# Alternating the next block's transposes with an output group, moving two f tiles ahead, and loading the first x tile in two parts

## The chip, the cores and the metric

One core of a Trainium2 chip. The metric is the device time of the kernel in microseconds, of one launch. The engines are PE (TensorE), PEld (its weight loads), DVE (VectorE), ACT (ScalarE), POOL (GpSimd) and SP (SyncE, which issues most loads and stores).

## The reference, cut to what matters

```python
w = softmax(weight_gen, axis=-1)                  # (8, 4096, 8 heads, 7 taps)
x_unf = windows of x over 7 tokens (6 before)     # (8, 4096, 7, 8, 24)
conv = einsum('bshk,bskhg->bshg', w, x_unf)       # 32768 tokens x 192
h = conv @ w_in                                   # 192 -> 2048
out = (h - tanh(h)) @ w_out                       # 2048 -> 192
```

## The kernel before

32 blocks of 1,024 tokens. GpSimd multiplies x by the seven taps ("products"), a DMA adds half of them to the others (the "accumulation"), PE transposes and sums the products into PSUM (L233), ScalarE copies that to `convT`. Then come 16 "f tiles" of the first matmul (L257); each lands in one of three PSUM buffers, from which ScalarE makes the tanh and VectorE the difference. Eight "output groups" of the second matmul (L289) run for the block before, one after every two f tiles. The transposes use the same three buffers as the f tiles.

```python
psum_h = ctx.enter_context(tc.tile_pool(name="psum_h", bufs=3, space=bass.MemoryType.PSUM))
...
def gemm1(n, f):                       # one f tile
    ph = psum_h.tile([P, 2, HT], FP32, name="ph", tag="ph")
    ...                                # 6 matmuls, 3 per row half
    last_act[0] = nc.scalar.activation(out=th[:], in_=ph_f, func=ACT.Tanh)
    last_sub[0] = nc.vector.tensor_sub(gt[:], ph_f, th[:])
...
for n in range(NTOT):
    if n + 3 < NTOT:
        load_wg(n + 3)
        load_x(n + 3)                  # waits until POOL has freed the tile
    for p in range(J):
        gemm1(n, 2 * p)
        gemm1(n, 2 * p + 1)
        if n >= 1:
            gemm2((n - 1) * J + p)     # 16 f tiles, two matmuls each
        ...
        if n + 1 < NTOT:
            if p == (6 if n > 0 else 7):
                conv(n + 1, (0, 1))    # transposes of two chunks
            if p == (6 if n > 1 else 7):
                conv(n + 1, (2,))      # and of the third
```

The softmax here doesn't subtract the row's maximum and nothing guards it: scores larger than these inputs give would overflow.

## Time and profile before

| | before |
|---|---|
| time, median (lowest to highest) | 770.57 us (770.43 to 771.18) |
| profiled span | 768.73 us |
| PE, DVE, ACT, POOL busy | 96, 85, 83, 90% |
| a good steady block | 22.63 us |
| blocks 1, 2, 3 | 25.55, 24.09, 24.38 us |

The four costliest groups of the page (line, engine, operation, output from inputs, shapes, count, then busy time in us and mean ns of one, then idle time of the engine before them and what ended it):

```profile
L269 DVE TENSOR_TENSOR gt<-ph,th 128x1024 bf16<-128x1024 f32 x512 | 602.8, 1219 | 93.3 <-ACT th L267 92.7
L267 ACT ACTIVATE th<-ph 128x1024 f32<-128x1024 f32 x512 | 497.2, 1022 | 65.7 <-PE ph L257 64.9
L257 PE MATMUL ph<-convT,w_in 64*128 64x512 bf16 x3072 | 382.1, 378 | 7.5 <-DVE gt L269 5.0
L289 PE MATMUL obank<-w_out,gt 64*128 64x192 bf16 x7936 | 374.6, 243 | 2.9 <-issue 2.1
```

DVE and ACT wait in total for each other and for PE (93 and 66 us); PE hardly waits for anybody, 7.5 us in its largest group. PE is the bound; GpSimd, 90% busy, comes next, and the two engines that wait have over 10% to spare. The durations of single matmuls (378 and 243 ns) overlap and say nothing of the rate; the rate is read from starts.

### The profile page before, as it was taken

The page shows a single profiled execution, that of the slowest core. Times are in us where ns is not written, and L with a number is a line of the kernel's source. Part 1 is how long each engine was busy: PE and PEld are TensorE (multiplying, and loading weights), DVE is VectorE, ACT ScalarE, POOL GpSimd, SP SyncE. Part 2 cuts the span into 40 slices and gives each one's busy share as a digit, 9 for nine tenths or more (in the row PEclk, how much of TensorE's full clock was granted, in tenths as well). Part 3 has the DMA queues.
Part 4 walks back from the last instruction along what each step waited for, and adds up shares of the span by engine and source line. Part 5 has one row for each costly group of instructions (what it writes and reads, how often), then busy time and mean ns, then how long its engine had stood idle before and what let it go on. Part 6 is the DMA issues. An engine that isn't in the chain of part 4 may idle for free.

```text
span 768.7 us, 32330 instructions
## 1 busy us (share of the span) xinstructions
PE 736.7 (96%) x14784; PEld 583.1 (76%) x14784; DVE 652.9 (85%) x595; ACT 640.8 (83%) x865; POOL 695.2 (90%) x290
## 2 busy tenths in 40 slices
PE   2799999999999999999999999999999999999997
PEld 2377787777777777788777777777778777787777
DVE  5987888888898888889888888888888988888883
ACT  1777878888888888888888888888888888888883
POOL 5999999999999999999999999999999999999100
PEclk9999999999999999999999999999999999999999
DMA  7823776555677555577655557765556765542412
GB/s 209 184 81 87 182 181 150 118 145 147 169 182 174 131 129 148 150 180 182 164 123 133 150 160 182 180 128 137 143 150 172 182 181 115 125 142 72 98 43 84
DMA packets 25847, 111.37 MB, mean 145 GB/s; under 512 B 4800, under 2 KB 9456, under 8 KB 21624
## 3 DMA queue, kind: packets, MB, share of 16 engines
q1 hardware_dynamic: 14688, 76.95, 29.9%
q0 software_dynamic: 10816, 31.99, 25.8%
q8 instruction: 115, 1.88, 1.0%
q10 hardware_dynamic: 208, 0.39, 0.2%
q14 instruction: 20, 0.16, 0.1%
HBM read 54.49 MB, written 25.17 MB: 104 GB/s over the span
## 4 chain that ended last, share of the span: by engine, by line
PE 93%; DVE 2%; issue 1%; POOL 1%; DMA 1%; ACT 1%; SPq 0%; POOLq 0%
PE ph L257 43%; PE obank L289 43%; PE pc L233 6%; DVE gt L269 2%; PE po L323 1%; DMA x_t<-in_x_dram 1%; POOL even L192 1%; ACT th L267 0%; ACT convT L244 0%; POOL odd L192 0%; DVE zr L151 0%; DVE zsum L145 0%; SPq L117 0%; SPq L93 0%; SPq L121 0%
## 5 line engine op out<-in xcount | busy, mean ns | idle before, releaser
L269 DVE TENSOR_TENSOR gt<-ph,th 128x1024 bf16<-128x1024 f32 x512 | 602.8, 1219 | 93.3 <-ACT th L267 92.7
L267 ACT ACTIVATE th<-ph 128x1024 f32<-128x1024 f32 x512 | 497.2, 1022 | 65.7 <-PE ph L257 64.9
L257 PE MATMUL ph<-convT,w_in 64*128 64x512 bf16 x3072 | 382.1, 378 | 7.5 <-DVE gt L269 5.0
L289 PEld LDWEIGHTS <-gt 64*128 64x128 bf16 x7936 | 345.1, 94 | 53.4 <-issue 2.5
L289 PE MATMUL obank<-w_out,gt 64*128 64x192 bf16 x7936 | 374.6, 243 | 2.9 <-issue 2.1
L192 POOL TENSOR_TENSOR even<-x_t,wsm 128x1536 bf16<-128x1536 f32 x94 | 272.8, 2903 | 3.9 <-DMA x_t<-in_x_dram 1.6
L192 POOL TENSOR_TENSOR odd<-x_t,wsm 128x1536 bf16<-128x1536 f32 x93 | 269.9, 2903 | 0.0
L257 PEld LDWEIGHTS <-w_in 64*128 64x128 bf16 x3072 | 180.1, 94 | 108.4 <-issue 11.8
L192 POOL TENSOR_TENSOR last<-x_t,wsm 128x1536 bf16<-128x1536 f32 x31 | 103.4, 3336 | 0.0
L307 ACT ACTIVATE out_sb<-obank 128x192 f32<-128x192 f32 x248 | 81.9, 330 | 10.5 <-PE obank L289 4.6
L244 ACT ACTIVATE convT<-pc 128x1024 bf16<-128x1024 f32 x64 | 48.9, 808 | 31.6 <-PE pc L233 31.5
L233 PE MATMUL pc<-ident,even 64*128 64x64 bf16 x2304 | 47.9, 192 | 2.9 <-POOL even L192 1.5
L233 PEld LDWEIGHTS <-even 64*128 64x128 bf16 x2304 | 42.7, 96 | 4.1 <-issue 2.2
L201 POOL DMA_DIRECT2D even<-odd x29 | 34.9, 1205 | 9.1 <-POOL odd L192 9.1
L163 POOL TENSOR_TENSOR wsm<-e_t,zr 128x448 f32<-128x448 f32 x30 | 41.7, 1390 | 0.0
L233 PE MATMUL pc<-ident,odd 64*128 64x64 bf16 x448 | 15.5, 198 | 13.1 <-DVE odd L192 12.8
L135 ACT ACTIVATE e_t<-wg_t 128x448 f32<-128x448 f32 x32 | 18.5, 578 | 8.2 <-DMA wg_t<-in_weight_gen_dram 8.2
L233 PE MATMUL pc<-ident,last 64*128 64x64 bf16 x768 | 23.3, 192 | 1.8 <-issue 1.7
L145 DVE TENSOR_REDUCE zsum<-e_t 128x64 f32<-128x448 f32 x32 | 19.5, 609 | 2.9 <-ACT e_t L135 2.9
L233 PEld LDWEIGHTS <-odd 64*128 64x128 bf16 x448 | 11.3, 100 | 13.6 <-DVE odd L192 12.9
L151 DVE RECIPROCAL zr<-zsum 128x64 f32<-128x64 f32 x30 | 16.6, 553 | 3.0
L233 PEld LDWEIGHTS <-last 64*128 64x128 bf16 x768 | 17.0, 96 | 2.2 <-issue 1.8
(20 smaller groups left out, 48.7 us busy)
## 6 DMA issues: line engine op xcount, KB each, us to landing
x_t<-in_x_dram SPq DMA_DIRECT2D x24, 1344.0 KB
even<-odd POOLq DMA_DIRECT2D x29, 1024.0 KB, 8.8
out_dram<-out_sb SPq DMA_DIRECT2D x31, 768.0 KB
x_t<-in_x_dram SPq DMA_DIRECT2D x8, 1176.0 KB
wg_t<-in_weight_gen_dram SPq DMA_DIRECT2D x32, 224.0 KB
x_t<-in_x_dram SPq DMA_DIRECT2D x8, 157.5 KB
w_in<-in_moe_w_in_dram POOLq DMA_DIRECT2D x6, 128.0 KB, 7.5
w_out<-in_moe_w_out_dram POOLq DMA_DIRECT2D x1, 768.0 KB, 10.8
```

What stands on the lines that cost most here:

```text
L135: nc.scalar.activation(out=e_t[:].rearrange("p j h k -> p (j h k)"), in_=wg_t[:].rearrange("p j h k -> p (j h k)"), func=ACT.Exp,)
L145: nc.vector.reduce_sum(out=zsum[:], in_=e_t[:].rearrange("p j h k -> p (j h) k"), axis=AX.X)
L163: return eng.tensor_mul(wsm.rearrange("p j h k -> p (j h) k"), e_t[:].rearrange("p j h k -> p (j h) k"), zr.rearrange("p (n o) -> p n o", ...
L192: eng.tensor_mul(dst[k].rearrange("p c j h g -> p j h c g"), x_t[:, k : k + J, :].rearrange("p j (h c g) -> p j h c g", h=H, c=NC), w[:, : ...
L201: nc.gpsimd.dma_start(out=even[:].rearrange("p i c j h g -> p (i c j h g)")[:, 0:ACC], in_=odd[:].rearrange("p i c j h g -> p (i c j h g)" ...
L233: nc.tensor.matmul(pc[:, r, col : col + R], lhsT=prods[c][gi][r * R : (r + 1) * R, c, 2 * j : 2 * j + 2].rearrange("p j h g -> p (j h g)") ...
L244: nc.scalar.activation(out=convT[:, c0 : c0 + nch, :].rearrange("p c (j r t) -> p r (c j) t", r=2, t=R), in_=pc[:, :, 0 : nch * JH * R].re ...
L257: nc.tensor.matmul(ph[:, r, :], lhsT=w_in[r * R : (r + 1) * R, c, f * P : (f + 1) * P], rhs=convT[r * R : (r + 1) * R, c, :], start=(c == ...
L267: last_act[0] = nc.scalar.activation(out=th[:], in_=ph_f, func=ACT.Tanh)
L269: last_sub[0] = nc.vector.tensor_sub(gt[:], ph_f, th[:])
L289: mm = nc.tensor.matmul(po[:, 0:D], lhsT=g_of[n][f][r * R : (r + 1) * R, col : col + P], rhs=w_out[r * R : (r + 1) * R, f, :], start=(r == ...
L307: last_act[0] = nc.scalar.activation(out=out_sb[:, j, :], in_=po[:, 0:D], func=ACT.Copy)
```

## The change

The intent: fill the short stop of PE ahead of f tile 14 with work that is ready (two f tiles of the next output group), spread the transposes among an output group's matmuls, and start the first products before the halo rows of x have arrived. The core of the diff:

```diff
+        if n == 0:
+            rows(0, P, HALO, HALO + J)      # 8 rows without halo first
+            rows(16, P, 0, HALO)
+            rows(1, 16, 0, HALO)
+            no_halo()
...
-    FA = 8 * P
+    FA = 7 * P                              # first part of w_in
...
-        on_vector=(3, 4, 5, 6),
-        sums=(3, 0, 4, 5, 1, 6, 2),
+        on_vector=(6, 3, 4, 5),
+        order_of=(6, 0, 3, 1, 4, 5, 2),
+        sums=(6, 3, 0, 4, 5, 1, 2),
...
+    LEAD, MIX, FILL = 6, 5, 2
...
-            if n >= 1:
+            if n >= 1 and (p < 6 or n == NTOT - 1):
                 gemm2((n - 1) * J + p)
...
+            if 1 <= n < NTOT - 1 and p == 6:
+                pcs = []
+                sums = conv_sums(n + 1, ((0, 1),), pcs)
+                gemm2((n - 1) * J + 6,
+                    between=lambda f: [next(sums, None) for _ in range(0 if f < LEAD else MIX)])
+                for _ in sums:
+                    pass
+                conv_out(n + 1, ((0, 1),), pcs)
+                conv(n + 1, (2,))
+                gemm2((n - 1) * J + 7, 0, FILL)
...
+            if 1 <= n < NTOT - 1 and p == 7:
+                gemm2((n - 1) * J + 7, FILL, NFT)
```

In block 1 the third chunk's transposes thereby also move from behind the last output group to the others.

More of the change, by code (lines that the diff above doesn't have):

```diff
@@ L103, in load_x, with rows @@
         x_t = xpool.tile([P, HALO + J, D], FP32, name="x_t")
-        def rows(p0, p1):
-            win = x[b, s0 + p0 * J - HALO : s0 + p0 * J - HALO + 1]
+        def rows(p0, p1, r0=0, r1=HALO + J):
+            win = x[b, s0 + p0 * J - HALO + r0 : s0 + p0 * J - HALO + r0 + 1]
             nc.sync.dma_start(
-                out=x_t[p0:p1, :, :],
+                out=x_t[p0:p1, r0:r1, :],
                 in_=bass.AP(
@@ L111, in rows, with no_halo @@
                     offset=win.offset,
-                    ap=[[J * D, p1 - p0], [D, HALO + J], [1, D]],
+                    ap=[[J * D, p1 - p0], [D, r1 - r0], [1, D]],
                 ),
             )
-        if s == 0:
+        def no_halo():
             nc.sync.dma_start(
@@ L120, in load_x @@
             )
-            nc.sync.dma_start(
-                out=x_t[0:1, HALO : HALO + J, :],
-                in_=x[b, 0:J].rearrange("(p j) d -> p j d", p=1),
-            )
+        if n == 0:
[3 more added lines that the diff above has]
+            no_halo()
+        elif s == 0:
+            no_halo()
+            rows(0, 1, HALO, HALO + J)
             rows(1, 16)
@@ L167, in scale, with products @@
         )
-    def products(n, on_vector=(), sums=None, hooks={}, behind=None):
+    def products(n, on_vector=(), order_of=None, sums=None, hooks={}, behind=None):
         x_t = x_of.pop(n)
@@ L189, in products @@
             hooks[-1]()
-        for k in range(K):
+        for k in order_of or range(K):
             eng, w = (nc.vector, wsm_v) if k in on_vector else (nc.gpsimd, wsm[:])
@@ L215, in products, with conv_sums @@
             prods_of[n] = [[dst[k] for k in (sums or range(K))]] * NC
-    def conv(n, *parts):
+    def conv_sums(n, parts, pcs):
         prods = prods_of[n]
@@ L221, in conv @@
             conv_of[n] = cpool.tile([P, NC, HT], BF16, name="convT")
-        convT = conv_of[n]
-        pcs = [psum_h.tile([P, 2, HT], FP32, name="pc", tag="ph") for _ in parts]
+        pcs.extend(psum_h.tile([P, 2, HT], FP32, name="pc", tag="ph") for _ in parts)
+        if parts[-1][-1] == NC - 1:
+            prods_of.pop(n)
         for gi in range(max(len(g) for g in prods)):
@@ L241, in conv, with conv_out @@
                             )
+                            yield
+    def conv_out(n, parts, pcs):
         for chunks, pc in zip(parts, pcs):
@@ L244, in conv @@
             nc.scalar.activation(
-                out=convT[:, c0 : c0 + nch, :].rearrange("p c (j r t) -> p r (c j) t", r=2, t=R),
+                out=conv_of[n][:, c0 : c0 + nch, :].rearrange(
+                    "p c (j r t) -> p r (c j) t", r=2, t=R
+                ),
                 in_=pc[:, :, 0 : nch * JH * R].rearrange("p r (cj t) -> p r cj t", t=R),
@@ L248, in conv @@
             )
-        if parts[-1][-1] == NC - 1:
-            prods_of.pop(n)
+    def conv(n, *parts):
+        pcs = []
+        for _ in conv_sums(n, parts, pcs):
+            pass
+        conv_out(n, parts, pcs)
     def gemm1(n, f):
@@ L266, in gemm1 @@
         g1_act[0] = last_act.get(0)
+        gt = gpool.tile([P, TOK], BF16, name=f"gt{f}", tag=f"gt{f}")
         last_act[0] = nc.scalar.activation(out=th[:], in_=ph_f, func=ACT.Tanh)
-        gt = gpool.tile([P, TOK], BF16, name=f"gt{f}", tag=f"gt{f}")
         last_sub[0] = nc.vector.tensor_sub(gt[:], ph_f, th[:])
@@ L272, with gemm2 @@
     LAST = (NTOT - 1) * J
+    LEAD, MIX, FILL = 6, 5, 2
     half = {}
     out_of = {}
-    def gemm2(i):
+    def gemm2(i, f0=0, f1=NFT, between=lambda f: None):
         ops = []
@@ L282, in gemm2 @@
             n, j = divmod(blk, J)
-            if r == 0:
+            if r == 0 and f0 == 0:
                 half[blk] = obank[blk % 2]
             ops.append((r, n, j, half[blk]))
-        for f in range(NFT):
+        for f in range(f0, f1):
             for r, n, j, po in ops:
@@ L299, in gemm2 @@
                     order(mm, g1_act[0] if i == 1 else last_act[0], "row tiles in one bank")
-        if i > 0:
+            between(f)
+        if i > 0 and f1 == NFT:
             blk = i - 1
@@ L360, in load_w_in @@
                 in_=bass.AP(
-                    tensor=src.tensor, offset=src.offset, ap=[[G * F, H], [F, GC], [1, f1 - f0]]
+                    tensor=src.tensor,
+                    offset=src.offset,
+                    ap=[[G * F, H], [F, GC], [1, f1 - f0]],
                 ),
@@ L409 @@
                 products(n + 2, behind=last_sub[0] if n > 1 else None)
-            if n + 1 < NTOT:
-                if p == (6 if n > 0 else 7):
-                    conv(n + 1, (0, 1))
-                if p == (6 if n > 1 else 7):
-                    conv(n + 1, (2,))
+            if n == 0 and p == 7:
+                conv(1, (0, 1))
+                conv(1, (2,))
+            if 1 <= n < NTOT - 1 and p == 6:
+                pcs = []
+                sums = conv_sums(n + 1, ((0, 1),), pcs)
+                gemm2(
+                    (n - 1) * J + 6,
+                    between=lambda f: [next(sums, None) for _ in range(0 if f < LEAD else MIX)],
+                )
+                for _ in sums:
+                    pass
+                conv_out(n + 1, ((0, 1),), pcs)
+                conv(n + 1, (2,))
+                gemm2((n - 1) * J + 7, 0, FILL)
             if n == 0 and p == 2:
```

## The prediction

> **What bounds the kernel now.** I read the page first, then the chain of waits, then the timeline of one steady block instruction by instruction, then the list of waits and the first 50 us. The kernel works through 32 blocks of 1,024 tokens. A block has 16 f tiles (first matmul, L257, into one of three two-bank buffers that ScalarE's tanh and VectorE's subtraction empty), eight output groups of the second matmul (L289, 16 f tiles each, for the block before) and the transposes of the next block (L233, into two of the same three buffers).
>
> ```profile
> PE 736.7 (96%) x14784; PEld 583.1 (76%) x14784; DVE 652.9 (85%) x595; ACT 640.8 (83%) x865; POOL 695.2 (90%) x290
> PE 93%; DVE 2%; issue 1%; POOL 1%; DMA 1%; ACT 1%; SPq 0%; POOLq 0%
> 388.18:410.81 22.63, 22.61 (x457) 17.96 (x456) 19.93 (x19) 19.93 (x28) 22.25 (x10) 1.00 0.61 155
> ```
>
> The first two lines are busy time and the chain by engine; the third is one steady block (stretch, length, busy PE, PE loads, DVE, ACT, POOL, clock, DMA share, GB/s). PE carries 93% of the chain, and in that block it has work in flight for 22.61 of 22.63 us. POOL, at 22.25 us, is almost as full. So the first question is how near PE is to its own floor. From the starts in the timeline, a pair of matmuls (one per row half) takes 216 ns at 512 columns, 82.5 ns at 192 and 29.2 ns at 64. A block holds 48, 128 and 52 such pairs: 48 x 0.216 + 128 x 0.0825 + 52 x 0.0292 = 10.37 + 10.56 + 1.52 = 22.45 us. Only 0.18 us of 22.63 is left to win in a good block. It sits here:
>
> ```profile
> 407.35 1.94 ACT L267 ACTIVATE th<-ph 128x1024 f32<-128x1024 f32 x2
> 408.40 2.35 DVE L269 TENSOR_TENSOR gt<-ph,th 128x1024 bf16<-128x1024 f32 x2 [0.26 <-ACT th L267]
> 410.25 1.51 ACT L244 ACTIVATE convT<-pc 128x1024 bf16<-128x1024 f32 x2 [0.60 <-PE pc L233]
> 410.50 0.30 PE L233 MATMUL pc<-ident,odd 64*128 64x64 bf16 x8
> 410.81 1.47 PE L257 MATMUL ph<-convT,w_in 64*128 64x512 bf16 x12
> 411.67 1.02 ACT L267 ACTIVATE th<-ph 128x1024 f32<-128x1024 f32 x1
> ```
>
> (Start, length, engine, work.) The last eight transposes start at 410.50 and need 4 x 29 ns = 0.12 us, but f tile 14 starts at 410.81: 0.19 us late. Its buffer is the one of tile 13, whose subtraction ends at 408.40 + 2.35 = 410.75. The page's idle list hardly shows this, since matmul ends are modelled and the last transposes cover the gap. I find the same gap of 0.19 us in 22 of the 30 inner blocks.
>
> A second loss is in the early blocks, where the period is 25.55, 24.09 and 24.38 us (blocks 1, 2, 3) instead of 22.63:
>
> ```profile
> 112.84 0.33 PE L233 MATMUL pc<-ident,last 64*128 64x64 bf16 x8
> 114.82 0.26 PE L233 MATMUL pc<-ident,last 64*128 64x64 bf16 x6 [1.65 <-issue]
> ```
>
> PE stands for 1.65 us on "issue", that is for nothing the profile can name. Counting PE's instructions up to each of these stops puts every one of them at 193 plus a multiple of 256, and a 16 KB packet of the instruction queue lands about 1.3 us before PE resumes. There are ten, 7.6 us in all, 4.4 of it in blocks 1 to 3.
>
> Third, the start:
>
> ```profile
> 2.86 7.30 DMA x_t<-in_x_dram
> 10.32 2.90 POOL even L192
> 13.23 1.55 POOL odd L192
> 16.05 2.90 POOL even L192
> ```
>
> This is the chain: the whole first x tile lands at 10.16, POOL then makes three products one after another (2.87 us apart), and the first f tile starts at 20.73.
>
> **What the Trainium skill says.** "TensorE: Matmul & The Clock Gate", section Back-to-back issue gap, gives N / 2.4 + 2.5 ns: 215.8, 82.5 and 29.2 ns for these widths. The trace agrees to the nanosecond, so the transposes are already at their floor and alternating them with wider matmuls cannot shorten them. Its Part 3, The mechanism, says that matmuls start and end in strict order and only the loads of different row groups overlap; the change's five transposes per f tile is an odd number, so the two row halves change places each time, and I cannot see in the kernel before what that costs. "Runtime: NRT & Kernel Launch", Instruction fetch mechanics, says instructions come in 16 KiB blocks of 256, fetched while the current one runs, "mostly hidden". The trace agrees on the size and shows it not hidden: 1.84 us between matmuls at the worst.
>
> **The change part by part.** Instruction counts are equal (29,570 rows on PE in both), so only order and waits change.
>
> 1. Start. The first DMA of x is now the 8 rows without halo for all partitions (786 KB), issued at about 1.2 instead of 2.86 us, then the 6 halo rows, then the zeros. Product 6 needs no halo and moves to the front of VectorE; POOL still starts with product 0, which needs everything. The same 1.38 MB flowed at about 1.365 MB in 5.4 us before (3.2 to 8.6). Starting as soon as the first weights are in (2.8), it should be through 0.4 to 1.3 us sooner: POOL at about 9.3 instead of 10.32, so -1.0 us. The three POOL products remain in series, so product 6 coming early buys VectorE 1.7 us but not the chain. The first w_in part (7 instead of 8 tiles) is there to keep pace: its copy landed at 20.81, behind the first tile; with 7/8 of the bytes (3.7 us x 1/8 = 0.5) and less in front of it, it should land near 19.6. The price: tile 7 now needs the second part. That landed at 30.2; with 9/8 of the bytes and an issue 1 us earlier I get 29.7, while tile 7 would like to start at 28.5. Tile 7's subtraction was due only at 32.78 - 1.0, and its matmul, tanh and waits take 1.93 us, so up to 29.85 nothing is lost. Close. I count -1.0 for the start, with 0 to -1.4 possible.
>
> 2. Block 1. Its chunk 2 transposes now stand with the others rather than just before block 2's first f tile, which waited 0.52 us for their eviction: -0.5 us.
>
> 3. Steady blocks. The two leading f tiles of the next output group (2 x 82.5 = 0.165 us) fill the 0.19 us gap. But f tile 14 does not start earlier: from tile 12 to tile 14 the trace needs 0.87 (to tanh) + 1.05 (to the subtraction) + 1.14 + 1.21 (two subtractions) + 0.06 = 4.33 us, which is just what it took (406.48 to 410.81). What is saved comes after tile 14, when 0.165 us of matmuls is already done. There the next limit waits: tile 1 of the next block reuses tile 14's buffer, and that round trip takes 0.87 + 1.06 + 1.22 + 0.06 = 3.21 us. Before, PE had 3.26 us of work between the two (410.81 to 414.07). After: 3.26 - 0.165 = 3.10. So PE stands 0.11 us there instead, and the block gains 0.05, less perhaps 0.02 because the output copy of the mixed group reaches ScalarE later and pushes the two evictions ahead of tanh 14, which has no slack. 0.03 x 28 blocks = 0.8 us.
>
> 4. Alternation. 50 of 64 transposes move up among f tiles 6 to 15. Total PE work is equal; the last of them still ends about 2.26 us after the group begins, so both evictions come at the same time as before. Zero by itself. The spacing of instruction blocks hardly changes either (256 instructions at the densest place take about 2.5 us in both orders), so I expect about as many fetch stops, at other places.
>
> Sum: 770.5 - 1.0 - 0.5 - 0.8 = 768.2; I say 768.0.
>
> **The rivals.** (a) The whole gap goes: if tile 1's round trip is hidden better than I think, 28 x 0.18 = 5 us more: 763. For it: the filler's length fits the gap so well. Against it: the 3.21 us round trip, which every step meets with just 0.05 us to spare. (b) The odd five costs time: in strict order with a skew between halves (19 and 10 ns in the trace), each change of parity could lose 10 to 15 ns, ten times a block, 0.1 to 0.15 us, and that comes before tile 14, on the chain: 28 x 0.1 = 3 us, 770 to 771. (c) The fetch stops fall elsewhere: up to 3 us either way. (d) POOL becomes the bound: its wsm starts come 22.64 to 22.66 us apart with no wait, so PE cannot run faster than that for long. The third block's accumulated products land about 84.6, its transposes began at 87.0 and now begin 0.8 earlier; that leaves 1.6 us of lead. This caps (a) at about 763 too. (e) Tile 7 waits for w_in and eats the start's gain: 769.
>
> **Range and chances.** Together they leave 764 to 771 for 8 in 10: (a) with good fetches at the lower end, (b) with (e) at the upper. Two per cent would be 15 us; PE's floor, 32 x 22.45 us = 718 plus start and end, allows about that only if all stops vanish. So within 2%: 0.97; faster 0.02; slower 0.01.
>
> **What would show it.** Right: first POOL product near 9.3 us; first f tile near 19.7; no gap before tile 14 beyond the filler, but a stop of about 0.1 us before tile 1 of the next block, behind the subtraction; good periods near 22.60; stops at 256-instruction steps still there. Wrong: good periods of 22.45 (rival a) or 22.7 and more with wider spacing in the mixed stretch (b); POOL named as releaser of transposes in steady blocks (d); VectorE idle over 0.5 us before subtraction 7 (e).

## The result, and the profile after

768.99 us (768.85 to 769.51, four runs) against 770.57 us: ratio 0.9979, 95% interval 0.9962 to 0.9996. Ratios here are the mean time of one kernel's fast runs over that of the other's of the same rounds, so not quite the ratio of the quoted medians. The change saves 1.6 us, 0.2%: the same within 2%. 2.5 us were predicted.

The page, the chain by engine, and one good block (stretch, length, busy PE, PEld, DVE, ACT, POOL, clock, DMA share, GB/s) of the changed kernel:

```profile
PE 737.2 (96%) x14784; PEld 577.8 (75%) x14784; DVE 652.8 (85%) x595; ACT 637.1 (83%) x865; POOL 695.3 (91%) x290
PE 93%; DVE 3%; POOL 1%; issue 1%; DMA 1%; ACT 0%; SPq 0%; POOLq 0%
...
367.61:390.19 22.58, 22.58 (x462) 17.89 (x459) 19.93 (x19) 19.80 (x28) 22.20 (x10) 1.00 0.62 156
```

Nothing has changed in kind: PE is the bound. This block is 22.58 us; the median of the good ones is 22.56. Where the gain of 0.07 us a block comes from can be read from the timeline of PE and DVE at the end of that block (start, length, engine, work):

```profile
386.47 1.22 DVE L285 TENSOR_TENSOR gt<-ph,th 128x1024 bf16<-128x1024 f32 x1
387.42 0.30 PE L240 MATMUL pc<-ident,odd 64*128 64x64 bf16 x8
387.54 0.35 PE L306 MATMUL obank<-w_out,gt 64*128 64x192 bf16 x4
387.74 1.47 PE L273 MATMUL ph<-convT,w_in 64*128 64x512 bf16 x12
389.65 2.35 DVE L285 TENSOR_TENSOR gt<-ph,th 128x1024 bf16<-128x1024 f32 x2 [0.79 <-ACT th L284]
390.19 1.57 PE L273 MATMUL ph<-convT,w_in 64*128 64x512 bf16 x12
```

The subtraction of tile 13 ends at 386.47 + 1.22 = 387.69; f tile 14 starts at 387.74, and the gap before it now holds the four matmuls of the two early f tiles (387.54). The stop has moved on to the last line, f tiles 0 and 1 of the next block: 12 matmuls take 1.57 us there. In the kernel before the same line was

```profile
413.42 1.48 PE L257 MATMUL ph<-convT,w_in 64*128 64x512 bf16 x12
```

so 0.09 us shorter. Over all blocks the step from the last matmul of tile 0 to the first of tile 1 has a median of 0.297 us after and 0.197 us before: PE waits 0.10 us for tile 14's buffer, whose subtraction (the first of the pair from 389.65) ends at about 390.85.

The start, from the chain in order of time:

```profile
2.66 6.70 DMA x_t<-zero
9.53 2.90 POOL even L197
12.43 1.66 POOL odd L197
15.26 2.91 POOL even L197
```

POOL starts at 9.53 instead of 10.32. The last piece to land is the zero row, now issued last. In block 1 the kernel before has a stop for no named reason:

```profile
68.20 0.90 PE L289 MATMUL obank<-w_out,gt 64*128 64x192 bf16 x17 [1.33 <-issue]
```

In the changed kernel PE stops there for longer, among the transposes:

```profile
64.10 0.19 PE L240 MATMUL pc<-ident,odd 64*128 64x64 bf16 x1
67.46 0.31 PE L240 MATMUL pc<-ident,odd 64*128 64x64 bf16 x5 [3.17 <-issue]
...
67.70:71.10 3.40, 3.40 (x47) 1.91 (x43) 0.00 (x0) 1.62 (x2) 3.40 (x2) 0.53 0.02 5
```

The last line, a stretch of the windows view, has a granted clock of 0.53: after the stop PE ran 3.4 us at half clock (67.50 to 70.91 in the clock record of the trace), and pairs of matmuls of f tiles 14 and 15 took 427 instead of 216 ns. The start of f tile 0 in some blocks, and the spans, put the whole account together (us, from matmul starts in the traces):

| start of f tile 0 of | before | after | after less before |
|---|---|---|---|
| block 0 | 20.73 | 19.94 | -0.79 |
| block 1 | 44.14 | 43.06 | -1.08 |
| block 2 | 69.69 | 72.15 | +2.46 |
| block 4 | 118.16 | 117.57 | -0.59 |
| block 31 | 731.41 | 730.18 | -1.24 |
| span | 768.73 | 767.60 | -1.13 |

1.08 us came from the start. Block 1 lost 3.54 (29.10 instead of 25.55). Blocks 2 and 3 gave 3.05 back: their fetch stops were gone or smaller (0.44 us in all instead of 2.88), and block 2 no longer waited for an eviction. Blocks 4 to 30 brought 0.65, though 27 good blocks at 0.07 would make 1.9. The profiled run of the changed kernel was the slowest of its four, 769.51 us.

**The stops.** I numbered PE's instructions in each trace (matmuls, weight loads and the few semaphore rows, in order of their starts) and set the packets of the instruction queue beside them. Counted from block 1 to block 30 as steps of more than 0.28 us between two PE instructions at number 193 + 256 k, there are 8 in the kernel before (7.5 us) and 10 in the changed one (7.7 us). In blocks 4 to 30 alone they sum to 3.0 us before and 3.9 us after. The other long steps are waits for a buffer or the half-clocked pairs. The four boundaries around block 1, my own count from the traces (us):

```
                  boundary passed   packet starts   lands   next boundary resumes   stop
before, no. 1473       63.30            65.82       66.90          68.20            1.57
after,  no. 1473       61.92            65.07       66.15          67.46            3.36
after,  no. 1217       55.57            55.75       56.98          61.92            none
after,  no. 1985       75.85            75.16       76.29          83.26            none
```

For each boundary a 16 KB packet brings the block of 256 instructions that begins at the next one. It mostly starts after PE has started the boundary's first instruction; for one boundary in eight it starts up to 0.7 us before that, as in the last row. It mostly takes 0.9 to 1.4 us, and where PE is stopped it resumes 1.2 to 1.6 us after the landing. Around number 1473 the packet started 2.5 and 3.15 us late; in the packet records the 10,752-byte packets of an x load and then the 1,792-byte packets of a weight load fill the DMA engines until just then. In the kernel before, 42 of the 115 packets start over 2 us late; packets of an x load were under way meanwhile for 35 of these, but only for 4 of the other 73. Around the transposes, PE's densest stretch, it runs through 256 instructions in 3.3 us before and 2.2 us after (7.4 us is the median of each trace). So my theory: **the middle of the change works as computed, but fetch stops behind x loads take its gain**. The rivals: that the alternation or the early f tiles are worth nothing, that GpSimd sets the pace, or that the stops belong to the transposes.

### The profile page after: what moved, and what is told of

Its sections match the earlier page's. It is cut to its first block, busy times and chain, and to the rows that moved or that the text cites. A ratio compares the mean times of both kernels' runs of the same rounds, so it can differ in the third digit from the quotient of the medians.

```text
span 767.6 us, 32329 instructions
## 1 busy us (share of the span) xinstructions
PE 737.2 (96%) x14784; PEld 577.8 (75%) x14784; DVE 652.8 (85%) x595; ACT 637.1 (83%) x865; POOL 695.3 (91%) x290
## 4 chain that ended last, share of the span: by engine, by line
PE 93%; DVE 3%; POOL 1%; issue 1%; DMA 1%; ACT 0%; SPq 0%; POOLq 0%
PE obank L306 43%; PE ph L273 43%; PE pc L240 6%; DVE gt L285 2%; PE po L341 1%; DMA x_t<-zero 1%; POOL even L197 1%; ACT th L284 0%; POOL odd L197 0%; SPq L107 0%; DVE zr L156 0%; DVE zsum L150 0%; ACT convT L254 0%; SPq L93 0%; DVE out_sb L353 0%
## 5 line engine op out<-in xcount | busy, mean ns | idle before, releaser
L306 PE MATMUL obank<-w_out,gt 64*128 64x192 bf16 x7936 | 399.2, 243 | 1.4 <-issue 0.6
L306 PEld LDWEIGHTS <-gt 64*128 64x128 bf16 x7936 | 351.4, 94 | 52.6 <-issue 1.2
L273 PEld LDWEIGHTS <-w_in 64*128 64x128 bf16 x3072 | 176.4, 94 | 112.1 <-issue 18.8
L240 PE MATMUL pc<-ident,even 64*128 64x64 bf16 x2304 | 70.3, 191 | 3.7 <-POOL even L197 2.4
L240 PEld LDWEIGHTS <-even 64*128 64x128 bf16 x2304 | 64.7, 96 | 5.0 <-POOL even L197 2.7
L240 PE MATMUL pc<-ident,last 64*128 64x64 bf16 x768 | 23.2, 192 | 8.5 <-DVE last L197 8.3
```

Of the source, the lines that this page charges most:

```text
L240: nc.tensor.matmul(pc[:, r, col : col + R], lhsT=prods[c][gi][r * R : (r + 1) * R, c, 2 * j : 2 * j + 2].rearrange("p j h g -> p (j h g)") ...
L273: nc.tensor.matmul(ph[:, r, :], lhsT=w_in[r * R : (r + 1) * R, c, f * P : (f + 1) * P], rhs=convT[r * R : (r + 1) * R, c, :], start=(c == ...
L306: mm = nc.tensor.matmul(po[:, 0:D], lhsT=g_of[n][f][r * R : (r + 1) * R, col : col + P], rhs=w_out[r * R : (r + 1) * R, f, :], start=(r == ...
```

## The experiments

Twelve kernels ran, all correct, in five rounds of timing each; four or five fast runs of each are used. Times are medians, with the ratio to the kernel before of the same rounds; "stops" are those at fetch boundaries as defined above, "good block" is the median period in the trace (in e45_late_load_filler small stops lift it; its undisturbed blocks take 22.45 to 22.47).

| run | us | ratio (95% interval) | good block | block 1 | stops: sum, count |
|---|---|---|---|---|---|
| (changed kernel) | 768.99 | 0.9979 (0.9962 to 0.9996) | 22.57 | 29.10 | 7.7, 10 |
| e1_start_only | 768.93 | 0.9974 (0.9961 to 0.9988) | 22.63 | 25.76 | 6.9, 8 |
| e2_no_fill | 769.01 | 0.9975 (0.9962 to 0.9987) | 22.63 | 29.02 | 6.1, 5 |
| e3_no_mix | 768.20 | 0.9966 (0.9954 to 0.9979) | 22.56 | 26.97 | 6.8, 6 |
| e5_second_filler | 768.34 | 0.9964 (0.9951 to 0.9976) | 22.47 | 29.00 | 9.3, 10 |
| e8_old_block1 | 768.68 | 0.9977 (0.9964 to 0.9989) | 22.58 | 24.91 | 7.2, 9 |
| e4_late_load | 768.73 | 0.9980 (0.9967 to 0.9992) | 22.56 | 24.69 | 5.1, 6 |
| e6_shift | 769.32 | 0.9981 (0.9968 to 0.9995) | 22.57 | 25.92 | 5.4, 7 |
| e45_late_load_filler | 767.65 | 0.9962 (0.9949 to 0.9974) | 22.56 | 24.89 | 6.9, 10 |
| e9_hold_loads | 763.49 | 0.9903 (0.9889 to 0.9918) | 22.56 | 25.03 | 2.7, 4 |
| e10_hold_filler | 762.87 | 0.9892 (0.9876 to 0.9909) | 22.47 | 24.99 | 5.1, 7 |
| e11_hold_old_middle | 765.07 | 0.9927 (0.9914 to 0.9941) | 22.63 | 24.14 | 1.6, 1 |
| e12_hold_no_mix | 763.79 | 0.9910 (0.9897 to 0.9924) | 22.56 | 25.07 | 3.3, 6 |

**The start alone (e1_start_only).** The changed kernel with the loop of the kernel before:

```diff
-            if n >= 1 and (p < 6 or n == NTOT - 1):
+            if n >= 1:
                 gemm2((n - 1) * J + p)
...                                   # and the old two conv() calls
```

> The kernel before with only the new start (first x tile without halo, product 6 first, w_in parts of 7 and 9 tiles). My theory: the start alone is worth what the changed trace shows at the first tile of block 1, 44.14 to 43.06, so 1.1 us, and the steady blocks keep the old period of 22.63 with 0.19 us before f tile 14. Total about 769.5, give or take 1.5 us of fetch stops that fall elsewhere. Rival: the start's gain is all there is in the whole change, then this equals the changed kernel, 769.0. A second rival: the start's gain is given back in block 1, and the total stays at 770.5.

It takes the time of the whole change, 768.93 us. The good blocks are the old 22.63. So the timed gain of the change can be had from the start alone, which is what the first rival said; but the table shows why the rest does not appear: with the old order block 1 takes 25.76 us, and the trace is at block 4 at 116.74, 0.83 ahead of the changed kernel.

**Without the early f tiles (e2_no_fill).**

```diff
-    LEAD, MIX, FILL = 6, 5, 2
+    LEAD, MIX, FILL = 6, 5, 0
```

> The changed kernel with no f tile of the next output group put ahead of f tile 14. My theory (two round trips of the buffers limit a block): the wait moves back to tile 14 (0.19 us), the 0.19 us before tile 1 of the next block goes, and good blocks take 22.63 us again instead of 22.56: 28 x 0.07 = 2 us slower than the changed kernel in the good blocks, about 771. Rival: the alternation is what shortened the block; then the period stays at 22.56.

The period went to 22.63 as expected, and the two medians went back to those before (step before tile 14: 0.207 us; before tile 1: 0.197). The two f tiles are the whole of the 0.07 us. The total did not become 771: this trace has five stops instead of ten, 1.6 us less. A gain of 2 us cannot be seen in the total as long as the stops vary by as much.

**Without alternation (e3_no_mix).**

```diff
-    LEAD, MIX, FILL = 6, 5, 2
+    LEAD, MIX, FILL = 6, 0, 2
```

> The changed kernel with the transposes in one piece after the output group (the two f tiles still ahead of tile 14). My theory: alternation costs and gains nothing on the engine, since ten transposes and two f tile pairs take 311 ns in the changed trace against 310 by the floors; good blocks stay at 22.56, and the total within 1 us of the changed kernel apart from fetch stops that move. Rival: alternation shortens the block by giving the evictions an earlier start; then good blocks are longer by 0.03 us or more here. Other rival: alternation thins out the instruction stream and saves stops; then the stops in the first blocks are larger here.

Good blocks 22.56, the total 0.8 us lower, with overlapping intervals. Alternation does not shorten a block. The stop in block 1 is 2.88 us and no half clock follows it. Whether alternation thins out the stops stays unclear: without it those of blocks 1 to 3 sum to 4.9 us instead of 3.8, but all of them to 6.8 instead of 7.7.

**A second filler (e5_second_filler).**

```diff
             gemm1(n, 2 * p)
+            f0 = FILL if n >= 2 and p == 0 else 0
+            if f0:
+                gemm2((n - 1) * J, 0, f0)
             gemm1(n, 2 * p + 1)
...
-                gemm2((n - 1) * J + p)
+                gemm2((n - 1) * J + p, f0, NFT)
```

> The changed kernel with, in addition, the first two f tiles of the first output group between f tile 0 and f tile 1 of every block from 2 on. My theory: they fill the 0.19 us before tile 1 as the first pair filled the one before tile 14, and now nothing else is near: good blocks 22.56 - 0.165 = 22.40 us, 4.6 us less in all, about 764.4. Rival: GpSimd, whose blocks take 22.65 us without a wait, becomes the bound as soon as its lead is used up; then later blocks go to about 22.65 with transposes waiting for its products, and the gain is 2 us or less. Second rival: the next buffer's round trip (tile 0 to tile 3) takes the wait over, and the period stays at 22.56.

From PE's timeline of this run, at the boundary of two blocks (same columns as above):

```profile
389.00 0.83 PE L273 MATMUL ph<-convT,w_in 64*128 64x512 bf16 x6
389.65 0.34 PE L306 MATMUL obank<-w_out,gt 64*128 64x192 bf16 x4
389.81 0.83 PE L273 MATMUL ph<-convT,w_in 64*128 64x512 bf16 x6
```

Tile 0, the filler and tile 1 follow each other by their own rates (0.65 and 0.16 us): the stop before tile 1 is gone, and the good blocks are at 22.47, against 22.45 by PE's floors (22.40, as I had expected, is below the floor and was a slip). So the stop that ate over half of the first filler is the one named. The total fell only by 0.0015 of the time, with overlapping intervals: the stops rose to 9.3 us in this trace.

**Block 1 in the old order (e8_old_block1).**

```diff
-            if 1 <= n < NTOT - 1 and p == 6:
+            if n == 1 and p == 6:
+                conv(2, (0, 1))
+            if n == 1 and p == 7:
+                conv(2, (2,))
+            if 2 <= n < NTOT - 1 and p == 6:
```

> The changed kernel with block 1 alone in the old order (transposes in two pieces, no alternation, no early f tiles). My theory: the steady gain of 0.07 us a block is real and a single fetch stop in block 1, made worse by the new order there, ate it. Then block 1 goes from 29.1 back to 25.6 to 25.8 us as with the start alone, blocks 2 and 3 to 24.1 each if their stops come back (or stay near 22.5 and 23 if not), and the total is 766 to 768. Rival: the time from block 1 to block 4 is set by something else (GpSimd's products), so that what block 1 gives is lost in blocks 2 and 3: then block 4 starts at the same time as with the change (117.3 to 117.6) and the total stays at 769.

Block 1 fell to 24.91 us with a stop of 0.92. Yet the total is 768.68, a little above the range. Blocks 2 and 3 took 24.59 and 23.82, with stops of 1.71 and 1.33 us that the changed kernel had not or only in part (0.44). Of the 4.19 us that block 1 gained, they gave back 2.99; block 4 starts at 117.07, somewhat before the rival's 117.3. So the rival was mostly right in its effect, but not in its cause: GpSimd was not waited for. I take it that a stop avoided early shifts the blocks after it against the loads, so that another takes its place; no run shows this by itself.

**The fifth x tile loaded later (e4_late_load).**

```diff
-            load_x(n + 3)
+            if n != 1:
+                load_x(n + 3)
...
+            if n == 1 and p == 7:
+                load_x(4, behind=last_act[0])   # its first DMA waits for this tanh
```

> The changed kernel with the load of the fifth x tile held back until the tanh of the last f tile of block 1, so that it no longer runs while block 1's transposes go through. My theory: the fetch of the next 256 instructions waited behind that load's packets (it started at 65.07, when the load was almost done); without them it starts within 1.2 us of its boundary, so the stop in block 1 falls from 3.36 us to 1 us or less, the clock does not drop after it, and block 1 takes 23.5 to 25 us instead of 29.1: total 764.5 to 766. Rival: the stop has another cause (the order of the transposes, or the instruction queue itself); then it stays at 3 us and more, and the total at 769. Second rival: the later load makes GpSimd late, and the transposes of blocks 2 to 4 wait for products; then the gain is given back there.

The first transposes after the boundary in block 1:

```profile
64.51 0.24 PE L242 MATMUL pc<-ident,odd 64*128 64x64 bf16 x5 [0.41 <-issue]
```

The packet started 0.56 us after its boundary, not 3.15, and the stop is 0.60 us instead of 3.36; block 1 takes 24.69 us. That settles that the load made the fetch late. The total did not follow, and the second rival says why: the same delay pushed the load into the next accumulation, and PE stood 2.4 us before the transposes of block 2:

```profile
87.63 0.24 PE L242 MATMUL pc<-ident,even 64*128 64x64 bf16 x5 [2.25 <-DVE gt L287]
```

The profile names VectorE for this wait, but the accumulation, started at 74.23, landed only at 87.50. Another 1.5 us went in block 3, whose fetch stop was 1.92 instead of 0.44 us. The chain of the run with the filler and the same late load (e45_late_load_filler) shows it:

```profile
73.89 0.30 issue
74.19 13.31 DMA even<-odd
87.50 0.14 issue
```

The accumulation took 13.3 us; its median in the kernel before is 8.8.

**Both together (e45_late_load_filler).**

> The second filler (two f tiles between f tiles 0 and 1) and the late load of the fifth x tile together, as a version that could beat both kernels. My theory: the two gains add, 768.3 less the 3.5 to 4.5 us of the late load: 764 to 765, with good blocks at 22.47. Rival: GpSimd, whose blocks take 22.65 us, becomes the bound once PE has caught up with it: then the last blocks take 22.65 and the transposes wait for its products or for the accumulation; the total is then 765 to 766.5.

767.65 us: a miss for both theories. The wait in block 2 (2.3 us) and 6.9 us of other stops remained; the last blocks stayed at 22.46, so GpSimd was not the bound.

**Instruction boundaries shifted (e6_shift).** The result of these matmuls is never read.

```diff
+    pad = psum_h.tile([P, 2, HT], FP32, name="pad", tag="ph")
+    for _ in range(88):
+        nc.tensor.matmul(pad[:, 0, 0:R], lhsT=ident[:], rhs=ident[:, 0:R], start=True, stop=True)
```

> The changed kernel with 88 more small matmuls (176 PE instructions) at the very start, where PE waits for x; nothing else differs. Their result is never read. My theory (stops at the ends of fetched blocks of 256): all stops are still at 193 plus a multiple of 256 in the new count, so 176 instructions earlier in the program. Boundaries of block 1 then fall at the old instructions 1297 (57.7, before the load of the fifth x tile), 1553 (62.7) and 1809 (about 65): the stop moves from among the transposes to f tile 14 and is about 2.3 us instead of 3.36. Total 766 to 770, as other stops change as well. Rival: the stop belongs to the transposes themselves (a buffer, an eviction or the switch between groups): then it stays at the same transpose, at old instruction 1729, with 3.3 us.

All seven stops are at 193 + 256 k in the new count. In block 1 they are at the new numbers 1729 and 1985, the old 1553 and 1809, both foretold; at the old number 1729, where PE had stopped for 3.36 us, there is none. So the stops belong to instruction blocks, not to the transposes. The sizes were wrong (1.10 and 0.93 us instead of one of 2.3): this run started with 20 us at half clock, reached block 1 3.2 us later, and met the load at another point.

**All x loads held (e9_hold_loads).** Like e4_late_load, but every load from the fifth on waits for the tanh of f tile 13:

```diff
-            load_x(n + 3)
+            if n == 0:
+                load_x(n + 3)
...
+            if p == 6 and 1 <= n < NTOT - 3:
+                load_x(n + 3, behind=last_act[0])
```

> The changed kernel with every x load from the fifth on held back until the tanh of f tile 13 of its block, so that it starts as the transposes run and not some 10 us before them. My theory: the stops come from instruction fetches waiting behind such loads, and in the late-load run a later load of the fifth tile moved into the next accumulation, which took 13.3 us instead of 8.8 and made the transposes of block 2 wait. Held until tile 13 it should be over (about 71) before that accumulation starts (74). Then the stop in block 1 is under 1 us, block 2 keeps 22.6 to 23.5, the stops of blocks 3, 5 and 7 (0.4 to 1.9 us) mostly go, all stops sum to under 4 us instead of 9, and the total is 762 to 765. Rival: the stops only move, to the fetches after the transposes, and their sum stays at 7 us or more: total 767 to 769. Second rival: GpSimd's lead of 5 us at the last blocks is used up and the transposes wait for the accumulation: total no lower than 765.

763.49 us, 7.3 us below the median of the kernel before in the same rounds (770.84), within the expected 762 to 765. The place in block 1 that had the 3.17 us:

```profile
65.55 0.24 PE L242 MATMUL pc<-ident,odd 64*128 64x64 bf16 x5 [0.76 <-issue]
```

Four stops are left, 2.7 us. One of them is new, 1.02 us at number 1985: its packet now waits behind the held load and starts 5.2 us after the boundary, but PE is among f tiles there and slower to need it. In this trace the accumulated products were ready 0.8 us or more before the transposes of every block, so the second rival did not bind.

**With the second filler (e10_hold_filler).**

> The same with the second filler, as the version that could beat both kernels. My theory: good blocks at 22.47 on top, 28 x 0.095 = 2.6 us less than the run with held loads alone, unless GpSimd becomes the bound: 760 to 763. Rival: GpSimd's 22.65 us a block is the floor from the middle on: then the last blocks take 22.65 with the accumulation named as what the transposes wait for, and this equals the run with held loads alone.

762.87 us, the lowest median of all, by 0.0108 against the kernel before; 0.6 us better than held loads alone, not 2.6, and with overlapping intervals not clearly better. Good blocks are at 22.47. The list of PE's waits now has a line that the others have not:

```profile
PE pc L242 <- DMA even<-odd: 1.2, 1, 1.2
```

The transposes waited once for the accumulation, in block 28, which took 23.9 us. Blocks 20 (23.9 us) and 29 (23.2 us) were long for another reason, fetch stops of 0.88 and 0.69 and of 0.81 us. But the products landed only 0.15 and 0.47 us before the transposes of blocks 18 and 19 needed them, so GpSimd with its 22.65 us a block begins to bind, as the rival had it; the last blocks did not go to 22.65.

**The old middle with held loads (e11_hold_old_middle), and no alternation with held loads (e12_hold_no_mix).** Their edits are those of e1 and e3 on top of e9.

> The kernel with the new start and the old order in every block (as in the run of the start alone), with the x loads held back as in the run with held loads. My theory: with the large stops gone, the middle part of the change (early f tiles and alternation) shows its own worth, 0.07 us in each of 28 blocks: this takes 1.5 to 2.5 us more than the run with held loads on the changed kernel (763.5), so 765 to 766, with good blocks at 22.63. Rival: the middle part is worth nothing even then, and this is at 763.5 as well.

> The run with held loads on the changed kernel, without the alternation (the transposes in one piece, the two f tiles still early). My theory: with the stops gone, alternation is worth nothing: 763.5 within 0.7 us, good blocks at 22.56. Rival: alternation thins the instruction stream, so that more and longer stops come back without it: 764.5 or more, with a sum of stops over 5 us.

765.07 us with good blocks at 22.63: with most stops gone the middle of the change shows its worth in the total, 765.07 - 763.49 = 1.6 us by the medians (0.0024 by the ratios, 1.8 us; the intervals just overlap). Without alternation it is 763.79, the same as with it. That run shared its rounds with e11_hold_old_middle and differs from it by the early f tiles and by where chunk 2 stands in block 1: its slowest run (764.03) is below the fastest of the old middle (764.26).

## Why the prediction was right or wrong

The time lay in the range, 768.99 in 764 to 771, and 1.0 us above the point. That says little: the range also holds the time of no change, and the new start alone takes as long as the whole change. It is partly luck that the point was so near: the steady blocks gained more than I had put, and the stops, which I had left out of the sum, took that and more. The steps fared differently.

- **The bound and the floor: right.** The second filler brought the good blocks to 22.47 us against the 22.45 computed.
- **Part 1, the start: right.** -1.0 predicted, -0.79 at f tile 0 and -1.08 at block 1. POOL started at 9.53 (9.3 predicted), the w_in copy landed at 19.61 (19.6). The second w_in part landed at 28.23, earlier than the 29.7 I computed, and tile 7 started at 28.44: VectorE lost nothing and rival (e) is out. The first f tile varied from 19.2 to 20.3 us over the twelve experiments with this start, so single traces do not resolve it better than about 0.5 us; which of its three pieces brought how much was not tried.
- **Part 2, block 1: the wait right, the sum for the block wrong in sign.** The wait for the eviction went: a step of 0.63 us at the start of block 2 before, none over 0.28 us after. But the block's largest loss was a fetch stop of 1.57 us, and I took "about as many fetch stops, at other places" to mean that they cancel. What failed is the claim that the spacing of instruction blocks hardly changes. With chunk 2 among the other transposes PE ran from number 1473 to 1729 in 2.18 us instead of 3.33 (2.18 in e4_late_load too and 1.89 in e3_no_mix; 3.33 and 3.34 in e1_start_only and e8_old_block1, which keep the old order there), and the packet started 0.63 us later. The two make up the growth of the stop, from 1.57 to 3.36 us; with 3.4 us at half clock behind it, the block became 3.54 us longer. Blocks 2 and 3 gave most of it back, so that from block 1 to block 4 the sum was +0.49 us. e8_old_block1 and e4_late_load show that this block is bought back easily and most of the gain is lost again in the next ones.
- **Part 3, the steady blocks: the mechanism right, the size a little small.** The stop before tile 14 went, and one of 0.10 us came before tile 1 (0.11 predicted). Good blocks gained 0.07 us instead of 0.03 to 0.05: the deduction for ScalarE's later copy was not needed. e2_no_fill and e5_second_filler tell it apart from alternation. The sum of 0.8 us was not seen in blocks 4 to 30 (0.65) for this reason: they would have made 1.9, and stops took most of the rest (3.9 us there instead of 3.0). Rival (a) falls: good blocks took 22.57 us, not 22.45.
- **Part 4, alternation: right,** zero (e3_no_mix, e12_hold_no_mix). Rival (b) falls: ten transposes and two f tile pairs, over one change of parity and back, took 311 ns in the trace, just what the rates give (5 x 29.2 + 2 x 82.5).
- **Rival (c), the stops, was the larger matter.** It stood in the prediction with 3 us either way; holding the loads showed it to be worth some 5.5 us (768.99 less 763.49, of different rounds; 5.9 by the ratios). Most of these stops the kernel before had too.
- **Rival (d), GpSimd: not binding at this speed,** but just below it: it shows once in e10_hold_filler, at 762.9. That this is near the 763 that I had computed is luck: I had read the third block's transposes as beginning at 87.0, where the trace has 88.47, so GpSimd's lead there was 3.9 us and not 2.4, and the cap, reckoned again with it, would be some 1.5 us lower (an estimate).

Left open: in which place the instruction packet waits, in its queue or on an engine (the runs show only that it goes when the load is through), and why the sum of stops differs by up to 3 us between kernels whose steady order is nearly the same.

## What to carry to other kernels

When PE stops on nothing that the profile names, number its instructions: here the stops at a fixed step of 256 were late instruction fetches, and the large ones fell where the instructions are densest just after or during a bulk load. Moving the load, with a wait for something that happens during the dense stretch (the tanh of f tile 13), brought some 5.5 us here, more than three times the 1.6 us of the whole change; but see what the load collides with next. A filler in a wait is worth what the next wait leaves of it: follow the same buffer one round further before counting the gain.

## What the Trainium skill lacked or had wrong

- "Runtime: NRT & Kernel Launch", Instruction fetch mechanics: block size and count (16 KiB, 256 instructions) agree. "Mostly hidden" holds by the count, as 8 of 107 boundaries in blocks 1 to 30 of the kernel before have a stop over 0.28 us, but these cost 7.5 us, and one in the changed kernel 3.36 us; nothing warns of it. It gives PE 128 KiB, and the memory in general 2 lines; the runs fit the latter: a packet was fetched at about each boundary for the block behind the current one, and PE stopped at the end of the current one where that had not arrived. Missing: a packet mostly takes 0.9 to 1.4 us, and a stopped PE resumes 1.2 to 1.6 us after it lands.
- "DMA: Bandwidth & Descriptors", Queues, rings and completion order: it describes a round robin between queues at packet granularity. Here a fetch of one packet started up to 5.2 us after its boundary, as a load of 1.38 MB went through, and another 0.56 us after its boundary once the load ahead of it was moved. The page does not say that bulk loads delay instructions; whether the round robin itself is as described, no run here shows.
- "TensorE: Matmul & The Clock Gate", Part 3: it has nothing on matmuls of different widths alternating in two row groups; an odd count cost nothing (311 ns, as the rates give). Its Part 1 (half clock after an idle window of about 3.4 us) roughly agrees: half clock for 3.41 us after the stop of 3.36 us, in which PE was idle for 3.17, so a little less than the page's window was enough; none after a stop of 2.88 us.
